# Attention and gated MLP on one core: the last Wo products of each block moved behind most of the next block's down products, and layer norm steps tied to score steps without a value group

## The chip, the cores and the metric

The kernel runs on one core of a Trainium2 chip. The metric is device time in microseconds (us), the median of several runs. In the text, PE is TensorE (matmuls), DVE is VectorE, ACT is ScalarE, POOL is GpSimd. Gains in microseconds are differences of medians, unless the text says otherwise.

## The reference, cut to what matters

```python
def reference(A_x, A_wqkv, A_wo, B_x, B_w_gate, B_w_up, B_w_down):
    xn = _layernorm(A_x)                        # 2048 tokens x 512
    # attention: 32 heads of 16, causal, window of 256 keys
    #   p = softmax(mask(q @ k.T / 4)),  o = p @ v,  then  o @ wo
    # MLP: (xn @ w_gate) * (xn @ w_up) @ w_down, hidden size 1792
    return A_x + attention(xn) + mlp(xn)        # bf16, [1, 2048, 512]
```

## The kernel before

The tokens go in four chunks T of 512, each with four output blocks b of 128. Scores, exp, masks and values of attention are the backbone: 76 score steps, each for one of four head groups c of a chunk. All other TensorE work (projections, gate, up, down, Wo) is a list of fillers that a budget deals out between the score steps. One output block is one sum in a PSUM bank: 14 down products over the hidden size, then 4 Wo products, one for each head group (Wo 0 to Wo 3); then DVE adds x and stores. The value products of a head group (a value group) come two score steps after its last scores; so those of the last head group of a chunk come in the second score step of the next chunk.

```python
def divide(self, T, c):          # DVE, after the two transposes that end values()
    rz = ...;  nc.vector.reciprocal(out=rz[:], in_=at[:, :, :, 16])
    on = ...;  nc.vector.tensor_tensor(out=on..., in0=at[:, :, :, 0:16], in1=rz..., op=ALU.mult)
    nc.vector.transpose(out=self.OT[T][:, c, :], in_=on...)

def wo(self, T, b, cs):          # PE: needs OT of each head group c in cs
    for ps, c0, c1 in self.sums[b]:
        for c in cs:
            self.nc.tensor.matmul(ps, lhsT=self.OT[T][:, c, 128 * b:128 * b + 128],
                                  rhs=self.Wo[:, c, c0:c1], start=False, stop=(c == 3))
# ... in fillers(): the list; add(cost, function), cost in matmuls; norm steps cost 0
for T in range(NCH):
    todo = {}
    if T:
        todo = norms(T + 1, 0, 1) if T + 1 < NCH else {}
        for b in range(4):
            for g in todo.get(b, ()):
                add(*g)
            down(T - 1, b)
            wo(T - 1, b, (0, 1))
            wo(T - 1, b, (2, 3))
            add(0, lambda T=T, b=b: self.store(T - 1, b))
    for g in todo.get(4, ()):
        add(*g)
    gu(T, norms(1, 1, 3) if T == 0 else {})     # gate and up products
    if T + 1 < NCH:
        project(T + 1)
# ... in run(): one score step after another; values lag two steps behind
for g, s in enumerate(steps):
    fill(-1, g)
    valued = ready
    self.scores(*s)
    # ...
    if values(g - LAG):
        fill(min(spent + 4, upto), g)
        divide(g - LAG)
    if g < len(steps) - 1:
        fill(upto, g)
        self.mask_diag(*s)
# ... after the last score step
divide(len(steps) - 1)
valued = ready
fill(spent + 12, -1)
for b in range(3):
    self.wo(T, b, (3,))
    self.store(T, b, on_act=(b == 1))
```

The list is in order: if a Wo item is not yet allowed (its head group's `divide` has not been issued), the list stops there, and so does all filler work. PE and DVE keep to the program's order in the cases below: at 69.8 us, for instance, 14 down products whose inputs are long written start only behind a Wo product that waits. Matmul sums and value sums share a rotating pool of four PSUM banks (`ps_m`).

The softmax here doesn't subtract the row's maximum and nothing guards it: scores larger than these inputs give would overflow.

Of the kernel before, what the change touches and what calls it, by code (L numbers as in the profile page):

```python
# [25 lines left out]
class Kernel:  # L26
# [335 lines left out]
    def down(self, T, b, lo, hi):  # L362

        nc = self.nc
        if lo == 0:
            if T == self.NCH - 1 and b == 3:
                last = self.ps_m.tile([128, 256], F32, tag="M", name="psd3")
                self.sums[b] = [(self.late[3][:, 0:256], 0, 256), (last[:], 256, 512)]
            elif T == self.NCH - 1 and b == 2:
                self.sums[b] = [(self.late[2][:], 0, 512)]  # L370
            else:
                self.sums[b] = [(self.ps_m.tile([128, 512], F32, tag="M", name="psd")[:], 0, 512)]
        for f in range(lo, hi):
            for ps, c0, c1 in self.sums[b]:
                nc.tensor.matmul(ps, lhsT=self.hT[T][:, f, 128 * b:128 * b + 128],  # L375
                                 rhs=self.Wd[:, f, c0:c1], start=(f == 0), stop=False)

    def wo(self, T, b, cs):
# [4 lines that stand above are left out]
# [20 lines left out]
    def fillers(self):  # L403


        out = []
        NCH, NF = self.NCH, self.NF

        def add(cost, f, before=None, after=None):
            out.append((cost, f, before, after))  # L410

        halves = ((0, 1), (2, 3))

        def qk(T, c, before, which=(1, 0)):
            for is_k in which:
                for ks in halves:
                    add(2, lambda is_k=is_k, ks=ks: self.proj_qk(T, c, is_k, ks), before)

        def project(T):
            add(0, lambda: self.new_chunk(T))  # L420
            for b in range(4):
                for ks in halves:
                    add(2, lambda t=4 * T + b, ks=ks: self.proj_v(t, ks), self.first[T, 0])
            add(0, lambda: self.swap_halves(T, self.nc.sync), self.first[T, 0])
            for c in range(4):
                qk(T, c, self.first[T, c])

        def gu(T, between):
            for f in range(NF):
                for ks in halves:  # L430
                    add(2, lambda f=f, ks=ks: self.gate(T, f, ks))
                for ks in halves:
                    add(2, lambda f=f, ks=ks: self.up(T, f, ks))
                for g in between.get(f, ()):
                    add(*g)

        def norms(T, at, step):

            t, out = 4 * T, {}
            for b in range(4):  # L440
                for k, f in enumerate((lambda b=b: self.norm_stats(t + b, 1),
                                       lambda b=b: self.norm_scale(t + b, 1),
                                       lambda b=b: self.norm_apply(t + b),
                                       lambda b=b: self.norm_transpose(t + b, True))):
                    out.setdefault(at + step * b + (0, 0, 1, 1)[k], []).append((0, f))
            return out

        def down(T, b):
            for lo in range(0, NF, 2):
                add(2, lambda lo=lo: self.down(T, b, lo, lo + 2))  # L450

        def wo(T, b, cs):
            add(len(cs), lambda: self.wo(T, b, cs), None, self.last[T, cs[-1]])

        qk(0, 1, self.first[0, 1], (0,))
        for c in range(2, 4):
            qk(0, c, self.first[0, c])
        for T in range(NCH):
            todo = {}
            if T:  # L460
                todo = norms(T + 1, 0, 1) if T + 1 < NCH else {}
                for b in range(4):
                    for g in todo.get(b, ()):
                        add(*g)
                    down(T - 1, b)
                    wo(T - 1, b, (0, 1))
                    wo(T - 1, b, (2, 3))
                    add(0, lambda T=T, b=b: self.store(T - 1, b))
            for g in todo.get(4, ()):
                add(*g)  # L470
            gu(T, norms(1, 1, 3) if T == 0 else {})
            if T + 1 < NCH:
                project(T + 1)
        T = NCH - 1
        for b in range(4):
            down(T, b)
            if b < 3:
                wo(T, b, (0, 1, 2))
            if b in (1, 3):
                add(1, lambda b=b: self.add_x(T, b, 0 if b == 1 else 1))  # L480
        return [(*o, None, None)[:4] for o in out]

    def run(self):
        self.xns, self.stats, self.sums = {}, {}, {}
        self.act_free = False
        self.setup()
        NCH, LAG = self.NCH, 2
        RESERVE = 36
        self.first_chunk()
        steps, self.first, self.last = [], {}, {}  # L490
        for T in range(NCH):
            for c in range(4):
                self.first[T, c] = len(steps)
                for pieces in LATER if T else FIRST:
                    self.last[T, c] = len(steps)
                    steps.append((T, c, pieces))
        due = {g: key for key, g in self.last.items()}
        SCORES, VALUES = 1.85, 5.5
        work = self.fillers()
        total = sum(w[0] for w in work) - RESERVE + SCORES * len(steps) + VALUES * (len(due) - 1)  # L500
        spent, n, scored = 0, 0, 0
        valued, ready = -1, -1

        def fill(upto, group):
            nonlocal spent, n
            while n < len(work):
                cost, f, before, after = work[n]
                if after is not None and after > valued:
                    break
                if spent + cost / 2 > upto and not any(  # L510
                        w[2] is not None and w[2] <= group for w in work[n:]):
                    break
                self.act_free = spent + cost - scored >= ACT_FREE
                f()
                spent += cost
                n += 1

        def values(g):
            nonlocal spent
            if g not in due:  # L520
                return False
            self.values(*due[g])
            spent += VALUES
            return True

        def divide(g):
            nonlocal ready
            self.divide(*due[g])
            ready = g
# [5 lines that stand above are left out]
            scored = spent  # L535
            spent += SCORES
            upto = total * (g + 1) / len(steps)
            if values(g - LAG):
                fill(min(spent + 4, upto), g)
                divide(g - LAG)  # L540
            if g < len(steps) - 1:
                fill(upto, g)
                self.mask_diag(*s)
        T = NCH - 1
        self.ps_s.__exit__(None, None, None)
        late = self.ctx.enter_context(self.tc.tile_pool(name="ps_late", bufs=1, space=bass.MemoryType.PSUM))
        self.late = [late.tile([128, 512], F32, tag=f"L{i}", name=f"L{i}") for i in range(4)]
        fill(spent + 10, -1)
        self.mask_diag(*steps[-1])
        fill(spent + 10, -1)  # L550
        self.values(*due[len(steps) - 1], self.late)
        spent += VALUES
# [6 lines that stand above are left out]
        fill(10 ** 9, -1)  # L559
        assert n == len(work)  # L560
        self.wo(T, 3, (0, 1, 2, 3))
        self.store(T, 3, 0)
        self.store(T, 3, 1, True)
# [37 lines left out]
```

## Time and profile before

| | before |
|---|---|
| median time | 273.4 us |
| span in the profile | 271.6 us |
| PE, DVE, ACT, POOL busy | 96%, 67%, 63%, 42% |

Before the change, from the page: busy time by engine, and busy tenths of PE in 40 slices of 6.8 us each.

```profile
PE 261.7 (96%) x3886; PEld 120.2 (44%) x3886; DVE 182.3 (67%) x351; ACT 170.6 (63%) x131; POOL 113.4 (42%) x282
...
PE   7999999999799999999989999999999999999993
...
PE 86%; DVE 9%; DMA 2%; ACT 1%; SPq 0%; issue 0%; POOL 0%; DVEq 0%; POOLq 0%
```

The last line is the chain that ended last, followed back from the last instruction, with each engine's share of the span. PE fills the span, and the two slices below 9 in the middle (the 11th, from 68 us, and the 21st, from 136 us) are where it stands. Before the change, the view of waits (engine, line, what it waited for: us in total, times, longest):

```profile
PEld L381 <- DVE OT L333: 3.8, 3, 1.8
...
PE psd L381 <- DVE OT L333: 2.5, 3, 1.5
...
PE S L258 <- ACT P L265: 0.5, 1, 0.5
...
PE acc L313 <- DVE hT L360: 0.5, 1, 0.5
```

L381 is the Wo product, L333 the transpose that writes OT. Before the change, the timeline of PE at the first of the two slices (start, duration, instruction; in brackets the idle time before it, and what ended that):

```profile
68.31 0.60 PE L381 MATMUL psd<-Wo,OT 128*128 128x512 bf16 x2
69.42 0.25 PE L258 MATMUL S<-Q,K 16*64 16x128 bf16 x4 [0.51 <-ACT P L265]
...
69.78 0.39 PE L381 MATMUL psd<-Wo,OT 128*128 128x512 bf16 x1
71.66 0.39 PE L381 MATMUL psd<-Wo,OT 128*128 128x512 bf16 x1 [1.49 <-DVE OT L333]
71.89 3.19 PE L375 MATMUL psd<-Wd,hT 128*128 128x512 bf16 x14
...
135.58 0.82 PE L381 MATMUL psd<-Wo,OT 128*128 128x512 bf16 x3
137.12 0.39 PE L381 MATMUL psd<-Wo,OT 128*128 128x512 bf16 x1 [0.72 <-DVE OT L333]
```

and what DVE did meanwhile:

```profile
68.41 1.31 DVE L319 STREAM_TRANSPOSE at<-acc 128x512 f32<-128x512 f32 x2 [1.77 <-PE acc L313]
69.76 0.35 DVE L327 RECIPROCAL rz<-at 128x32 f32<-128x32 f32 x1
70.15 0.70 DVE L331 TENSOR_TENSOR on<-at,rz 128x512 bf16<-128x512 f32 x1
70.89 0.71 DVE L333 STREAM_TRANSPOSE OT<-on 128x512 bf16<-128x512 bf16 x1
```

The values of the last head group end at 68.4 us. The path through DVE ends at 70.89 + 0.71 = 71.60, and Wo of that group starts at 71.66. In these 3.2 us PE has two Wo products, a score step and one more Wo product to do.

How long a hole really is: the timeline's idle time is counted from the end of the matmul before, and that end is an estimate. The Trainium skill says so ("Perfetto Trace Analysis", Tensor Engine Instruction (MATMUL, LD_WEIGHTS)), and this trace agrees: a 128x512 matmul is drawn 380 to 390 ns long, while the next starts after 216 ns. So holes are measured here by start distance: from a matmul's start to the next one's, less the time that its columns take at this trace's pace (216 ns for 512 columns, fewer in proportion). By this measure the three holes above are 0.67, 1.66 and 0.89 us, 3.2 us in all, where the timeline shows 0.51, 1.49 and 0.72.

### The profile page before, as it was taken

How to read it: one execution, taken by the hardware profiler on the slowest of the kernel's cores; microseconds unless marked ns; L12 is line 12 of the kernel's file. 1: busy time of each engine (PE TensorE's matmuls, PEld its weight loads, DVE VectorE, ACT ScalarE, POOL GpSimd, SP SyncE). 2: the span in 40 equal slices, each digit the busy share in tenths (PEclk: the TensorE clock that was granted, in tenths of full speed). 3: DMA queues.
4: the chain of work that ended last, by engine and by line, in shares of the span. 5: the costliest groups of instructions: out<-in, count | busy, mean ns of one | idle time of the engine just before them, and what ended most of it. 6: DMA issues, size and time to landing. Idle time of an engine off the chain costs nothing.

```text
span 271.6 us, 8888 instructions
## 1 busy us (share of the span) xinstructions
PE 261.7 (96%) x3886; PEld 120.2 (44%) x3886; DVE 182.3 (67%) x351; ACT 170.6 (63%) x131; POOL 113.4 (42%) x282
## 2 busy tenths in 40 slices
PE   7999999999799999999989999999999999999993
PEld 6444444444344444444434444444444444444452
DVE  5377998876845959676665868857662675969160
ACT  3666757686456676769655676768765666675400
POOL 6123333434545443345545543545443354443400
PEclk9999999999999999999999999999999999999999
DMA  6999911110021100001012110000200000000001
GB/s 197 365 350 344 243 21 22 23 46 0 28 55 41 39 2 4 2 2 43 5 39 72 31 22 2 0 4 2 46 9 32 24 21 2 2 0 6 0 24 57
DMA packets 19351, 15.12 MB, mean 56 GB/s; under 512 B 7152, under 2 KB 19312, under 8 KB 19312
## 3 DMA queue, kind: packets, MB, share of 16 engines
q1 hardware_dynamic: 18480, 14.06, 17.9%
q8 instruction: 30, 0.49, 0.8%
q10 hardware_dynamic: 832, 0.49, 0.6%
q14 instruction: 9, 0.07, 0.1%
HBM read 9.70 MB, written 2.10 MB: 43 GB/s over the span
## 4 chain that ended last, share of the span: by engine, by line
PE 86%; DVE 9%; DMA 2%; ACT 1%; SPq 0%; issue 0%; POOL 0%; DVEq 0%; POOLq 0%
PE gp L342 17%; PE up L356 17%; PE psd L375 16%; PE qkp L209 10%; PE S L258 9%; PE acc L313 6%; PE psd L381 4%; PE vp L197 4%; DVE at L319 2%; DMA Wqkv<-in_A_wqkv_dram 2%; DVE hT L360 1%; DVE OT L333 1%; DVE on L331 1%; PE L L375 1%; DVE gsb L350 1%; ACT P L265 1%
## 5 line engine op out<-in xcount | busy, mean ns | idle before, releaser
L265 ACT ACTIVATE P<-S 128x2048 bf16<-128x2048 f32 x76 | 141.0, 1855 | 60.6 <-PE S L258 56.9
L137 POOL TENSOR_SCALAR_AFFINE_SELECT P<-P 64x256 bf16<-64x256 bf16 x224 | 96.8, 432 | 127.8 <-ACT P L265 117.2
L342 PE MATMUL gp<-xnT,Wg 128*128 128x512 bf16 x224 | 60.0, 380 | 0.1
L356 PE MATMUL up<-xnT,Wu 128*128 128x512 bf16 x224 | 59.6, 380 | 0.0
L375 PE MATMUL psd<-Wd,hT 128*128 128x512 bf16 (+1 forms) x210 | 50.3, 373 | 0.0
L360 DVE TENSOR_TENSOR hT<-up,gsb 128x512 bf16<-128x512 f32 x56 | 38.4, 686 | 16.3 <-PE up L356 14.4
L286 DVE TENSOR_TENSOR P<-P,diag 128x512 bf16<-128x512 bf16 (+1 forms) x76 | 30.6, 404 | 11.1 <-ACT P L265 11.1
L375 PEld LDWEIGHTS <-hT 128*128 128x128 bf16 x238 | 22.0, 98 | 24.4 <-issue 2.8
L319 DVE STREAM_TRANSPOSE at<-acc 128x512 f32<-128x512 f32 x30 | 19.7, 695 | 19.3 <-PE acc L313 19.3
L258 PE MATMUL S<-Q,K 16*64 16x320 bf16 (+2 forms) x720 | 31.1, 260 | 0.6 <-ACT P L265 0.5
L356 PEld LDWEIGHTS <-Wu 128*128 128x128 bf16 x224 | 20.4, 98 | 25.3 <-issue 2.5
L342 PEld LDWEIGHTS <-Wg 128*128 128x128 bf16 x224 | 20.3, 98 | 25.5 <-issue 2.7
L258 PE MATMUL S<-Q,Ko 32*64 32x320 bf16 (+1 forms) x720 | 31.1, 260 | 0.0
L209 PE MATMUL qkp<-xnT,Wqkv 128*128 128x512 bf16 x128 | 30.0, 380 | 0.0
L258 PEld LDWEIGHTS <-K 16*64 16x64 bf16 x720 | 12.3, 103 | 32.7 <-issue 32.7
L350 DVE CAST gsb<-gp 128x512 bf16<-128x512 f32 x36 | 24.5, 682 | 2.4 <-PE gp L342 1.0
L348 ACT ACTIVATE gsb<-gp 128x512 bf16<-128x512 f32 x20 | 11.9, 597 | 12.2 <-PE gp L342 11.5
L313 PE MATMUL acc<-P,VS 64*32 64x320 bf16 (+4 forms) x672 | 18.9, 254 | 0.0
L381 PE MATMUL psd<-Wo,OT 128*128 128x512 bf16 (+1 forms) x60 | 16.4, 374 | 2.5 <-DVE OT L333 2.5
L313 PE MATMUL acc<-P,V 64*32 64x320 bf16 (+4 forms) x672 | 18.4, 254 | 0.5 <-DVE hT L360 0.5
L209 PEld LDWEIGHTS <-Wqkv 128*128 128x128 bf16 x128 | 11.7, 98 | 14.5 <-issue 1.4
L399 DVE TENSOR_TENSOR y<-psd,x 128x512 bf16<-128x512 f32 x13 | 8.9, 688 | 13.3 <-PE psd L381 13.1
(54 smaller groups left out, 201.4 us busy)
## 6 DMA issues: line engine op xcount, KB each, us to landing
Wg<-in_B_w_gate_dram SPq DMA_DIRECT2D x2, 896.0 KB, 11.5
Wu<-in_B_w_up_dram SPq DMA_DIRECT2D x2, 896.0 KB, 12.8
Wd<-in_B_w_down_dram SPq DMA_DIRECT2D x1, 1792.0 KB, 17.6
out_dram<-y SPq DMA_DIRECT2D x14, 128.0 KB, 1.7
Wqkv<-in_A_wqkv_dram SPq DMA_DIRECT2D x3, 512.0 KB, 6.4
x<-in_A_x_dram SPq DMA_DIRECT2D x1, 1024.0 KB, 10.3
VS<-V SPq DMA_DIRECT2D x6, 144.0 KB, 2.6
x<-in_A_x_dram SPq DMA_DIRECT2D x1, 512.0 KB, 11.2
```

The costliest lines, as they stand in the source:

```text
L137: nc.gpsimd.affine_select(out=v, in_=v, pattern=pattern + [[1 if diag else -1, 64]], compare_op=ALU.is_ge if diag else ALU.is_gt, fill=0.0 ...
L209: nc.tensor.matmul(ps[:], lhsT=self.Wqkv[:, k, lo:lo + 128], rhs=self.xnT[T][:, :, k, :], start=(k == 0), stop=(k == 3))
L258: nc.tensor.matmul(S[64 * par:64 * par + 64, e, col:col + n], lhsT=(self.Ko if par else self.K)[U][rows, c, keys], rhs=self.Q[T][rows, c, ...
L265: nc.scalar.activation(out=P[:, :, 0:col], in_=S[:, :, 0:col], func=ACT.Exp, scale=0.25)
L286: self.nc.vector.tensor_tensor(out=v, in0=v, op=ALU.min, in1=self.diag.unsqueeze(1).unsqueeze(1).to_broadcast([128, 4, n, 64]))
L313: nc.tensor.matmul(accs[par][32 * e:32 * e + 32, q:q + n], lhsT=v, rhs=P[rows, e, col:col + n], start=(i == 0), stop=(i == len(todo) - 1), ...
L342: nc.tensor.matmul(ps[:], lhsT=self.Wg[:, k, 128 * f:128 * f + 128], rhs=self.xnT[T][:, :, k, :], start=(k == 0), stop=(k == 3))
L350: nc.vector.tensor_copy(out=self.gsb[:], in_=ps[:])
L356: nc.tensor.matmul(ps[:], lhsT=self.Wu[:, k, 128 * f:128 * f + 128], rhs=self.xnT[T][:, :, k, :], start=(k == 0), stop=(k == 3))
L360: nc.vector.tensor_tensor(out=self.hT[T][:, f, :], in0=ps[:], in1=self.gsb[:], op=ALU.mult)
L375: nc.tensor.matmul(ps, lhsT=self.hT[T][:, f, 128 * b:128 * b + 128], rhs=self.Wd[:, f, c0:c1], start=(f == 0), stop=False)
L381: self.nc.tensor.matmul(ps, lhsT=self.OT[T][:, c, 128 * b:128 * b + 128], rhs=self.Wo[:, c, c0:c1], start=False, stop=(c == 3))
```

## The change

Its intent: twelve of the next block's down products stand between the two halves of a block's Wo products, so that PE has work while DVE finishes OT. Before, the list stopped at the second half, which was not allowed yet, and at chunk 1 PE went into the score step after two Wo products alone; now four down products come between. And the norm steps of the next chunk leave the list and are tied to fixed score steps, leaving out the one with a value group (offset 1).

```diff
-        def down(T, b):
-            for lo in range(0, NF, 2):
+        def down(T, b, part=range(0, NF, 2)):
+            for lo in part:
                 add(2, lambda lo=lo: self.down(T, b, lo, lo + 2))
@@ fillers(), for each chunk
-            todo = {}
             if T:
-                todo = norms(T + 1, 0, 1) if T + 1 < NCH else {}
+                if T + 1 < NCH:
+                    for i, fs in norms(T + 1, 0, 1).items():
+                        self.beside[self.first[T, 0] + (0, 2, 3, 4, 5)[i]] = fs
+                down(T - 1, 0)
+                wo(T - 1, 0, (0, 1))
                 for b in range(4):
-                    for g in todo.get(b, ()):
-                        add(*g)
-                    down(T - 1, b)
-                    wo(T - 1, b, (0, 1))
+                    if b < 3:
+                        down(T - 1, b + 1, range(0, NF - 2, 2))
                     wo(T - 1, b, (2, 3))
                     add(0, lambda T=T, b=b: self.store(T - 1, b))
-            for g in todo.get(4, ()):
-                add(*g)
+                    if b < 3:
+                        down(T - 1, b + 1, range(NF - 2, NF, 2))
+                        wo(T - 1, b + 1, (0, 1))
@@ run(), in each score step, ahead of the last fill
+            for _, f in self.beside.get(g, ()):
+                f()
```

More of the change, by code (lines that the diff above doesn't have):

```diff
@@ L498, in run @@
         SCORES, VALUES = 1.85, 5.5
+        self.beside = {}
         work = self.fillers()
```

## The prediction

> **What bounds the kernel.** TensorE. The page gives PE 261.7 us busy of a 271.6 us span (96%), DVE 67%, ACT 63%; the chain of waits is 86% PE. The Trainium skill ("Perfetto Trace Analysis", Identifying the Most-Contended Engine) warns that matmul busy time is a poor measure, so I read start-to-start distances: a 128x512 matmul follows the last after 216 ns almost everywhere, the warm pace that the skill gives ("TensorE: Matmul & The Clock Gate", Wait — 56ns, not 53.3ns?: 215.7 ns); clock 1.000. So only holes in the matmul stream can be won back. Between start-up and tail there are few: 0.6 us at 42 us, and two at chunk boundaries:
> - 68.4 to 71.9 us (chunk 1): the timeline shows PE idle 0.51 us before a score step (for ACT's exp) and 1.49 us before the Wo product of head group 3, which waits for OT: after the last value product DVE does 1.31 us of transposes, 0.35 reciprocal, 0.69 multiply, 0.71 transpose, done 3.2 us later. By start distances the two holes are 0.67 and 1.66 us over the normal pace.
> - 136 to 137.1 us (chunk 2): the same wait, 0.72 us in the timeline, 0.88 by start distance.
> Chunk 3 (200 us) has no hole.
>
> **What the change does.** No instruction is added or removed. PE's order moves at the three chunk boundaries alone: twelve down products of block b+1 (12 x 216 ns = 2.6 us) now stand before Wo products 2 and 3 of block b. In chunk 1, after the values end at 68.4, come two Wo, four down, the score step, eight down, Wo 2, Wo 3. By the same durations the scores start at about 69.7, after exp ended (69.4), and Wo 3 is reached at about 71.8, just after OT is written (71.6): a margin of 0.2 us. In chunk 2 it is over 1 us. Score steps and fill budget are unchanged, since norm steps cost 0 in the list.
> Costs: two open sums hold two of four rotating PSUM banks, so a new sum may wait for an older one's store (0.69 us on DVE). In the built order these waits existed before or have a matmul group and a score step in between: at most 0.3 us in all. Norm steps move a few us, off the value step; DVE has slack there and their results are used some 40 us later: about zero.
>
> **Sum.** 0.67 + 1.66 + 0.88 = 3.2 us, all on the critical path, since PE alone has no slack. The end is unchanged. 273.4 - 3.2 = 270.2; with a little lost again **270.3 us, range 269.7 to 271.4**. Chances: faster by over 2% (under 268.0) 0.01, within 2% 0.98, slower 0.01.
>
> **What would show it right.** Span about 268.5; PE's idle time before Wo products on OT (2.5 us, 3 times) near zero; the slices near 68 and 136 us full; ACT's 4.2 us hole before the exp at 76 us gone; about 2.3 us gained by the end of chunk 1's boundary, another 0.9 by chunk 2's.
> **Wrong if** new holes appear before a block's first down product (bank waits on DVE stores), if score steps wait more for ACT, if Wo 3 of chunk 1 still waits some tenths, or if an earlier TensorE only runs into DVE in the gate/up stretch (3.8 of 4 us busy at 88 to 92 us): then the gain shrinks to 1 to 2 us.

## The result, and the profile after

| | before | after |
|---|---|---|
| median (range) | 273.42 (273.21 to 273.84), 4 runs | 270.32 (270.01 to 271.56), 4 runs |
| ratio | 1 | 0.989 (95%: 0.987 to 0.992) |
| profiled span | 271.6 us | 269.8 us |

A ratio is the mean time of one kernel's fast runs over that of the other's in the same rounds, so it is not quite the ratio of the medians. The gain is 3.1 us, or 1.1%: within 2%, and clear of the noise.

The profiled run of the changed kernel is its slowest one (271.56 us). After the change, the first projection matmul in PE's timeline, and the waits that concern the holes:

```profile
8.12 0.38 PE L197 MATMUL vp<-Wqkv,xnT 128*128 128x512 bf16 x1 [1.39 <-DMA Wqkv<-in_A_wqkv_dram]
```
```profile
PE vp L197 <- DMA Wqkv<-in_A_wqkv_dram: 1.4, 1, 1.4
...
PEld L381 <- DVE OT L333: 0.8, 1, 0.8
...
PE psd L381 <- DVE OT L333: 0.3, 1, 0.3
```

In this run the load of Wqkv came late, and the first projection started at 8.12 us, against 6.85 before and 6.58 in the profile of a second measurement of the changed kernel. The program up to that point is the same in both kernels, so this is not put down to the change. Counted from the first projection to the end of the span, it is 264.8 us before (271.6 - 6.85), 261.7 after (269.8 - 8.12) and 261.7 in the second measurement (268.3 - 6.58): 3.1 us less both times. The gain comes in two steps, as predicted (2.3 and 0.9 us): counted from the first projection, chunk 1's first gate product starts at 79.81 us before and at 77.58 and 77.67 in the two profiles of the changed kernel (2.1 to 2.2 less), chunk 2's at 145.74, 142.61 and 142.69 (3.1 less, so another 0.9).

After the change, PE's slices, the PE timeline at the same two boundaries, and DVE's at the first:

```profile
PE   7799999999999999999999999999999999999993
```
```profile
69.58 0.61 PE L381 MATMUL psd<-Wo,OT 128*128 128x512 bf16 x2
70.03 1.03 PE L375 MATMUL psd<-Wd,hT 128*128 128x512 bf16 x4
70.98 0.25 PE L258 MATMUL S<-Q,K 16*64 16x128 bf16 x4
...
71.35 1.90 PE L375 MATMUL psd<-Wd,hT 128*128 128x512 bf16 x8
73.08 0.59 PE L381 MATMUL psd<-Wo,OT 128*128 128x512 bf16 x2
...
134.62 0.61 PE L381 MATMUL psd<-Wo,OT 128*128 128x512 bf16 x2
135.06 2.75 PE L375 MATMUL psd<-Wd,hT 128*128 128x512 bf16 x12
...
138.11 0.60 PE L381 MATMUL psd<-Wo,OT 128*128 128x512 bf16 x2
```
```profile
72.17 0.71 DVE L333 STREAM_TRANSPOSE OT<-on 128x512 bf16<-128x512 bf16 x1
```

No brackets are left: PE does not stand at either boundary. OT is written at 72.17 + 0.71 = 72.88 us; Wo 2 starts at 73.08 and Wo 3 one matmul later, at about 73.30, 0.4 us after OT. By start distance no hole over 0.25 us is left between 45 and 259 us; the one of 0.63 us at 42 us (44 us in this profile) is still there. The one wait for OT that remains (0.3 us in the timeline, 0.49 by start distance, at 260 us) is at the end of the kernel, which the change does not touch.

### The profile page after: what moved, and what is told of

It is laid out like the page before. It is cut to its first block, busy times and chain, and to the rows that moved or that the text cites. A ratio compares the mean times of both kernels' runs of the same rounds, so it can differ in the third digit from the quotient of the medians.

```text
span 269.8 us, 8889 instructions
## 1 busy us (share of the span) xinstructions
PE 261.7 (97%) x3886; PEld 120.6 (45%) x3886; DVE 181.6 (67%) x351; ACT 170.5 (63%) x131; POOL 114.0 (42%) x282
## 4 chain that ended last, share of the span: by engine, by line
PE 88%; DVE 7%; DMA 2%; ACT 1%; SPq 0%; issue 0%; POOL 0%; DVEq 0%; POOLq 0%
PE gp L342 17%; PE up L356 17%; PE psd L375 17%; PE qkp L209 10%; PE S L258 9%; PE acc L313 6%; PE psd L381 5%; PE vp L197 4%; DMA Wqkv<-in_A_wqkv_dram 2%; DVE at L319 1%; DVE hT L360 1%; PE L L375 1%; DVE gsb L350 1%; ACT P L265 1%; DVE OT L333 1%; DVE on L331 1%
## 5 line engine op out<-in xcount | busy, mean ns | idle before, releaser
L375 PE MATMUL psd<-Wd,hT 128*128 128x512 bf16 (+1 forms) x210 | 51.1, 373 | 0.0
L258 PE MATMUL S<-Q,K 16*64 16x320 bf16 (+1 forms) x720 | 31.1, 260 | 0.1
L350 DVE CAST gsb<-gp 128x512 bf16<-128x512 f32 x36 | 24.5, 682 | 2.4 <-PE gp L342 1.0
L197 PE MATMUL vp<-Wqkv,xnT 128*128 128x512 bf16 x64 | 15.5, 380 | 1.4 <-DMA Wqkv<-in_A_wqkv_dram 1.4
```

Of the source, the lines that this page charges most:

```text
L258: nc.tensor.matmul(S[64 * par:64 * par + 64, e, col:col + n], lhsT=(self.Ko if par else self.K)[U][rows, c, keys], rhs=self.Q[T][rows, c, ...
L350: nc.vector.tensor_copy(out=self.gsb[:], in_=ps[:])
L375: nc.tensor.matmul(ps, lhsT=self.hT[T][:, f, 128 * b:128 * b + 128], rhs=self.Wd[:, f, c0:c1], start=(f == 0), stop=False)
```

## The experiments

All were timed in five rounds against the kernel before on the same chip; before was at 273.30 us in the first group, 273.37 in the second, 273.40 in the third. Theory A: the whole gain is TensorE no longer standing before the Wo products. Rival B: a part of it comes from moving the norm steps. A second rival is that merely parting the two halves of Wo is what helps.

### The norm steps alone

```diff
 (the changed kernel, with the list of before, less its norm steps)
+                for b in range(4):
+                    down(T - 1, b)
+                    wo(T - 1, b, (0, 1))
+                    wo(T - 1, b, (2, 3))
+                    add(0, lambda T=T, b=b: self.store(T - 1, b))
```

> The order of Wo and down products as before; only the norm steps are tied to score steps without a value group. Theory A (the whole gain is TensorE no longer standing before the Wo products that wait for OT): no gain, within 0.3 us of before (273.4), the idle time of Wo products on OT stays at 2.5 us. Rival B (moving the norm steps off the value step frees DVE and so part of the gain is theirs): at least 0.8 us faster, and the wait on OT shrinks to under 1.7 us.

Measured: 273.29 us, ratio 1.0015 (0.998 to 1.005). The same three holes: 0.67, 1.67 and 0.89 us. This experiment, from the view of waits:

```profile
PE psd L381 <- DVE OT L333: 2.5, 3, 1.5
```

By itself the move of the norm steps is worth nothing, and rival B falls in this form.

### The new order of products alone, norm steps in the list behind a block's store

```diff
 (the kernel before, with the new order of down and Wo)
                     add(0, lambda T=T, b=b: self.store(T - 1, b))
+                    for g in todo.get(b + 1, ()):
+                        add(*g)
                     if b < 3:
                         down(T - 1, b + 1, range(NF - 2, NF, 2))
                         wo(T - 1, b + 1, (0, 1))
```

> The new order of Wo and down products, norm steps left in the list, each after the store of a block, so never between a value group's transposes and its division in chunk 1. Theory A: the full gain, 3.1 us faster than before (270.1 to 270.6), no idle time before Wo products. Rival B: less than 2.3 us faster.

Measured: 270.71 us, ratio 0.990 (0.987 to 0.992), 2.6 us faster than before. Both holes at the boundaries are closed, but this is 0.5 us short of the 3.1 us expected. A new hole of 0.63 us by start distance appeared. This experiment, PE's timeline where it stands, and DVE's timeline before that:

```profile
153.32 1.02 PE L356 MATMUL up<-xnT,Wu 128*128 128x512 bf16 x4 [0.47 <-DVE y L399]
```
```profile
148.85 0.65 DVE L399 TENSOR_TENSOR y<-psd,x 128x512 bf16<-128x512 f32 x1
149.43 0.39 DVE L167 TENSOR_SCALAR xn<-x,mv,rs 128x512 bf16<-128x512 bf16 x1
149.74 0.69 DVE L148 BATCH_NORM_STATS2 st<-x 128x6 f32<-128x512 bf16 x1
150.46 0.18 DVE L149 BATCH_NORM_AGGREGATE mv<-st 128x2 f32<-128x6 f32 x1
150.55 0.32 DVE L327 RECIPROCAL rz<-at 128x32 f32<-128x32 f32 x1
...
152.59 0.68 DVE L399 TENSOR_TENSOR y<-psd,x 128x512 bf16<-128x512 f32 x1
```

The up product needs the PSUM bank that the second store (L399) frees, and that store is behind three norm instructions in DVE's queue (1.1 us, from 149.43 to 150.55). In the second measurement of the changed kernel the last two stores of this chunk follow with no norm step between:

```profile
148.39 0.65 DVE L399 TENSOR_TENSOR y<-psd,x 128x512 bf16<-128x512 f32 x1
148.97 0.33 DVE L327 RECIPROCAL rz<-at 128x32 f32<-128x32 f32 x1
...
151.00 0.68 DVE L399 TENSOR_TENSOR y<-psd,x 128x512 bf16<-128x512 f32 x1
```

So neither theory is right as stated. The reorder carries the gain, and the tie keeps a bank wait out that would have taken some tenths of it.

### The new order of products alone, norm steps ahead of a block's first down product

```diff
 (the new order, norm steps in the list)
                 for b in range(4):
+                    for g in todo.get(b + 1, ()):
+                        add(*g)
                     if b < 3:
                         down(T - 1, b + 1, range(0, NF - 2, 2))
```

> The new order of Wo and down products, norm steps left in the list just ahead of each block's first down product, so that in chunk 1 a norm application, statistics and their aggregate (0.40, 0.69, 0.18 us) stand between the transposes and the reciprocal. Theory A: OT comes 1.2 us later, twelve down products no longer cover it, and Wo 3 of chunk 1 waits about 0.8 us (Wo 3 is reached 0.4 us after OT in the changed kernel); in chunk 2 it is about covered. So 2.2 to 2.6 us faster than before, not 3.1. If the norm steps did not matter for this order, the full 3.1.

Measured: 270.64 us, ratio 0.990 (0.987 to 0.992), 2.7 us faster than before, a little more than the 2.2 to 2.6 expected. This experiment, DVE's timeline at chunk 1, and PE's:

```profile
68.67 1.31 DVE L319 STREAM_TRANSPOSE at<-acc 128x512 f32<-128x512 f32 x2 [1.77 <-PE acc L313]
69.91 0.37 DVE L167 TENSOR_SCALAR xn<-x,mv,rs 128x512 bf16<-128x512 bf16 x1
70.20 0.69 DVE L148 BATCH_NORM_STATS2 st<-x 128x6 f32<-128x512 bf16 x1
...
72.10 0.71 DVE L333 STREAM_TRANSPOSE OT<-on 128x512 bf16<-128x512 bf16 x1
```
```profile
72.87 0.39 PE L381 MATMUL psd<-Wo,OT 128*128 128x512 bf16 x1 [0.43 <-DVE OT L333]
```

The norm steps stand between the value group's transposes and its division, OT comes late, and Wo 3 waits 0.59 us by start distance (expected 0.8). Both ways of leaving the norm steps in the list cost about the same, for different reasons. The medians alone (270.71 and 270.64 against 270.3) would not show that cost: the intervals overlap, and the chips differ. The profiles do: from the start of the first projection to that of the last matmul it is 260.15 us before, 257.02 and 257.10 in the two profiles of the changed kernel, and 257.49 and 257.57 in these two, so 0.4 to 0.5 us more.

### The wait taken away, the order kept (wrong result)

```diff
-lhsT=self.OT[T][:, c, 128 * b:128 * b + 128],
+lhsT=self.OT[T][:, c - (c == 3 and T < self.NCH - 1), 128 * b:128 * b + 128],
```

> The kernel before, in its own order, but in chunks 0 to 2 the Wo product of head group 3 reads the OT of group 2, which is long done (wrong result on purpose). Theory A: the two waits on OT go (1.66 and 0.88 us by start distance), the short wait of a score step for exp at chunk 1 (0.67 us) stays: 2.5 us faster than before, 270.9. If the gain had come from the order of the products as such (banks, spacing of stores), little: under 1 us.

Measured: 270.73 us, ratio 0.990 (0.987 to 0.992), 2.6 us faster than before, with a wrong result as meant. Of the three holes only that of the score step (0.67 us, waiting for exp) is left. This experiment, PE's timeline at chunk 1:

```profile
69.45 0.25 PE L258 MATMUL S<-Q,K 16*64 16x128 bf16 x4 [0.51 <-ACT P L265]
...
69.81 0.61 PE L381 MATMUL psd<-Wo,OT 128*128 128x512 bf16 x2
```

In the old order, with nothing moved, PE's not waiting for OT is worth its two waits, 1.66 and 0.89 us (2.5 us together). The rest of the change's gain is, by subtraction, the score step's hole; no run closes that hole alone.

### Fewer products in front: four and eight instead of twelve

```diff
-                        down(T - 1, b + 1, range(0, NF - 2, 2))
+                        down(T - 1, b + 1, range(0, 4, 2))          # or (0, 8, 2)
 ...
-                        down(T - 1, b + 1, range(NF - 2, NF, 2))
+                        down(T - 1, b + 1, range(4, NF, 2))         # or (8, NF, 2)
```

Four:

> The changed kernel with four instead of twelve down products of the next block before Wo 2 and 3. Theory A (what counts is how much independent work stands before the wait): Wo 3 of chunk 1 is reached 8 x 0.216 = 1.73 us earlier than in the changed kernel (there 0.4 us after OT), so it waits about 1.3 us by start distance; chunk 2 next to nothing. 271.6, 1.3 us slower than the changed kernel; the hole before the score step (0.67 us) stays closed, as four products suffice for that. If merely parting the two halves of Wo were enough: the full gain, 270.3.

Eight:

> The changed kernel with eight down products before Wo 2 and 3. Theory A: Wo 3 of chunk 1 is reached 0.86 us earlier and waits about 0.5 us; chunk 2 nothing; 270.8, 0.5 us slower than the changed kernel, between it and the one with four.

The changed kernel, once more, in the same group:

> The changed kernel once more, on the same chip as the next three. 270.3, ratio to before 0.9885, no matmul hole at the chunk boundaries.

| down products in front | hole before Wo 3, chunk 1 | median | ratio to before (95%) |
|---|---|---|---|
| 4 | 1.38 us | 271.86 | 0.994 (0.992 to 0.995) |
| 8 | 0.51 us | 270.67 | 0.990 (0.989 to 0.992) |
| 12 (the change) | none | 270.34 | 0.989 (0.987 to 0.990) |

The two experiments, PE's timeline before Wo 3 of chunk 1, first with four, then with eight:

```profile
71.54 0.39 PE L381 MATMUL psd<-Wo,OT 128*128 128x512 bf16 x1 [1.21 <-DVE OT L333]
```
```profile
71.60 0.39 PE L381 MATMUL psd<-Wo,OT 128*128 128x512 bf16 x1 [0.34 <-DVE OT L333]
```

From eight to four products, 4 x 216 ns = 0.86 us of work leave the place before the wait, and the hole grows by 0.87 us (the means of the times by 0.95). Wo 3 starts when OT is there, not when its turn comes. Parting the halves is not what helps; the amount of work in front is. The score step's hole stays closed in both.

### Chunk 1 alone

```diff
+                if T > 1:
+                    (the list of before, less its norm steps)
+                else:
                     (the changed list)
```

> The changed kernel with the new order of Wo and down products at the boundary of chunk 1 alone, chunks 2 and 3 in the old order (norm steps tied throughout). Theory A: 0.67 + 1.66 = 2.3 us faster than before, 271.0 to 271.1, and the hole of 0.88 us at chunk 2 is back; chunk 3 stays without one, in the old order too.

Measured: 271.26 us, ratio 0.990 (0.987 to 0.993), 2.1 us faster than before (expected 2.3). The hole of chunk 2 is back at 0.89 us, and chunk 3 has no hole before a Wo product in its old order. This experiment, PE's timeline at chunk 2:

```profile
134.80 0.39 PE L381 MATMUL psd<-Wo,OT 128*128 128x512 bf16 x1 [0.72 <-DVE OT L333]
```

(The profiles of this third group lack 22 of 3886 matmul records, which look like small holes of one or more matmuls' length at other places; they are not counted.)

### The same means at the end of the kernel

```diff
-        fill(spent + 12, -1)
+        fill(spent + 16, -1)
         for b in range(3):
             self.wo(T, b, (3,))
```

> The changed kernel, and at the end of the kernel four more matmuls' worth of down products before the last three Wo products that wait for the last OT (there a hole of 0.49 us in both profiles). The same means against the same kind of wait: the hole closes, 0.4 to 0.5 us faster than the changed kernel, 269.8. Rival: the end hangs on the last stores and their DMAs, which start later by the added products, and the time stays within 0.2 us of the changed kernel.

Measured: 269.58 us, ratio to before 0.986 (0.985 to 0.988). Against the changed kernel in the same rounds the means are 269.70 and 270.38, a ratio of 0.9975, or 0.7 us, a little more than the hole. The hole is gone: the waits of this kernel have no line for a Wo product on OT. PE's timeline at the end of the kernel, first in the second measurement of the changed kernel, then in this experiment:

```profile
259.09 0.60 PE L381 MATMUL psd<-Wo,OT 128*128 128x512 bf16 x2 [0.33 <-DVE OT L333]
```
```profile
259.46 0.59 PE L381 MATMUL psd<-Wo,OT 128*128 128x512 bf16 x2
```

The profiled spans are 267.8 and 268.3 us, with the first projection at 6.58 us in both: 0.5 us, the size of the hole. The stores at the end did not take it back. This version beats both kernels.

### Norm steps of chunk 1 tied as well: two that failed

```diff
-            gu(T, norms(1, 1, 3) if T == 0 else {})
+            if T == 0:
+                for i, fs in norms(1, 0, 1).items():
+                    self.beside[(4, 6, 7, 8, 10)[i]] = fs      # second try: (6, 7, 8, 10, 11)
+            gu(T, {})
```

> The kernel with the longer cover at the end, and the norm steps of chunk 1 also tied to score steps without a value group (4, 6, 7, 8, 10), in place of the gate and up list. The matmul hole of 0.63 us at 42 us is there because the value group waits for a bank that DVE frees late, behind a norm application, a mask and a cast. If the norm steps cause the backlog: the hole shrinks by about 0.4 us, 269.2. If DVE is just full there (3.8 to 3.9 of 4 us busy) the hole stays or moves, and the time stays at 269.6.

> The same with the norm steps of chunk 1 two score steps later (6, 7, 8, 10, 11). They keep clear of the value steps, but the last transposed activations may come late for chunk 1's projections at 50 us: a new hole there of up to 1 us would show it. Else as the one before, 269.2 to 269.6.

Measured: 270.56 us (ratio to before 0.987, 0.984 to 0.991) and 272.94 us (0.998, 0.994 to 1.002), both slower than the 269.6 of the version that they were built on (timed on another chip, where before was at 273.37 and not 273.40). The first try, then the second, PE's timeline where it stands:

```profile
40.43 1.02 PE L356 MATMUL up<-xnT,Wu 128*128 128x512 bf16 x4 [0.51 <-DVE hT L360]
...
44.00 0.26 PE L313 MATMUL acc<-P,VS 64*32 64x192 bf16 x4 [0.90 <-DVE gsb L350]
```
```profile
56.78 1.04 PE L197 MATMUL vp<-Wqkv,xnT 128*128 128x512 bf16 x4 [1.88 <-DMA xnT<-xn]
```

In the first, the hole of 0.63 us at 42 us became two of 0.68 and 1.06 us by start distance. At the second of them, 1.2 us of norm steps (42.06 to 43.29 us in DVE's timeline) stand right before the cast L350 that PE waits for. In the second try, chunk 1's last transposed activations came 2 us late, where up to 1 us was feared, and two holes of 1.01 and 0.71 us stand at 43 us besides. DVE is nearly full there (3.86 of 4 us busy from 38 to 42 us in the kernel before), and tying the norm steps only moved the backlog. The hole at 42 us stays open.

## Why the prediction was right, point by point

- **Size.** 270.3 us was predicted, 270.32 measured. The sum was 0.67 + 1.66 + 0.88 = 3.2 us of holes; all three closed in the profile, and 3.1 us came. That the medians meet to 0.02 us is luck: the runs of the changed kernel spread from 270.01 to 271.56, and "a little lost again" (0.1 us) was not derived from anything.
- **The bound.** Right: every hole that the experiments opened or closed in the matmul stream came through to the time, if not always in full. Taking the two waits away without moving anything gave 2.6 us for 2.5 expected.
- **Margins.** Wo 3 of chunk 1 was said to come 0.2 us after OT; it came 0.4 us after. Thin indeed: eight products were not enough.
- **Score step.** Four down products before the score step close its wait for exp: right, also in the versions with four and eight.
- **Banks.** No new hole before a block's first down product: right for the change.
- **ACT.** Its idle time of 4.2 us before the exp at 76 us was said to go. It shrank to 1.66 us, still waiting for a score step; PE has no hole there any more, so the miss cost nothing.
- **The wait count.** I wrote that the idle time of Wo products on OT (2.5 us, 3 times) would be near zero. It is 0.3 us, once: the third wait was the one at the end of the kernel, which I had not told apart, and it was worth 0.5 us when the same means was used on it.
- **The norm steps.** "Worth about zero" holds alone (273.29 us). It is wrong for the change as a whole: with the new order of products, norm steps left in the list cost 0.3 to 0.4 us in the median, 0.4 to 0.5 us between first projection and last matmul, through a late OT or a late bank. I had weighed the two halves of the change one by one, and not asked what the one did to the place where the other stood.
- **The range.** One run (271.56) fell outside it; there the load of Wqkv was late at the start.

## What to carry to other kernels

When the bounding engine waits for a short chain on another engine, count the chain (here 3.2 us) and put independent work of at least that length in front of the wait; each piece short of it comes back as waiting time, one for one. If an ordered list deals out the work, look at everything that the list carries along, cheap items on other engines too, since they land in the same gap and can lengthen the very chain. Then look for the same wait elsewhere: here the end of the kernel had it too.

## What the Trainium skill lacked or had wrong

- "Perfetto Trace Analysis" (Tensor Engine Instruction) says that a matmul's end is an estimate, but not that idle time read from it is short: 0.51, 1.49 and 0.72 us in the timeline were 0.67, 1.66 and 0.89 us by start distance, and the 3.1 us that came is nearer to the latter sum (3.2) than to the former (2.7).
- "Perfetto Trace Analysis" (Matmuls, under Optimizing Tensor Performance) advises rotating PSUM banks, but not that a bank is held as long as its store stands behind other work in DVE's queue: with three norm instructions in front of the store, 0.63 us of PE's time.
- No page that I used gives the time from the end of a DVE write to the start of the weight load that waits for it: 0.05 us here (OT written at 71.60 us, the load started at 71.66; four such places gave 0.05 us each).
